# Turning the attention output by DMA for twelve tiles, with the low half on GpSimd

## The chip, the cores and the metric

The kernel runs on one core of one Trainium2 chip. The metric is the device time of one launch, in microseconds (us). The engines are named as the profile names them: PE (TensorE), DVE (VectorE), ACT (ScalarE), POOL (GpSimd) and SP (SyncE, which issues most of the DMAs); PEld is the loading of weights into PE.

## The reference

A transformer block on 2048 positions of width 512 in float32: attention over 8 keys, spaced two positions apart, in 32 heads of 16, then an MLP with a squared ReLU; each is preceded by a layer norm and followed by a residual add.

```python
qkv = layernorm(x) @ wqkv                    # 512 -> 3 * 512, 32 heads of 16
idx = pos[:, None] - arange(8)[None, :] * 2  # keys at s, s-2, ..., s-14
logits = einsum("bhsd,bhswd->bhsw", q, k[idx]) * 16 ** -0.5   # masked where idx < 0
o = einsum("bhsw,bhswd->bhsd", softmax(logits), v[idx])
h = x + o @ wo
r = relu(layernorm(h) @ w1 + b1)             # 512 -> 1792
out = h + (r * r) @ w2 + b2                  # 1792 -> 512
```

## The kernel before

**Tiles and halves.** The positions are 16 tiles of 128 (`t` = 0 to 15), in four groups of four (R = 4). Every matrix product is made of three products of half-precision parts: each operand is split into a high half (`hi`: a rounding copy on ACT, L147) and a low half (`lo`: operand minus high half, L150), and PE adds high x high, low x high and high x low in PSUM (`mm3`, 12 matmuls of 128x512 each). `lows_last` puts the products that need the low half of the first operand at the end, so that the eight others can go ahead of it.

**The chain of one tile.** Attention (DVE: products with the keys at L343, sums at L377, products with the values at L354, the latter added up on POOL by three instructions at L411) leaves its result `o`. This must be turned (transposed in blocks of 128x128) before `wo_product` can multiply it. There are two ways to turn it. `o_T` uses four PE transposes into PSUM. The other way goes by DMA: `o_split` copies the tile on ACT into two planes of 16 bits (`pl`, L594), `turn_dma` lets SP issue a transposing DMA (L598), and `o_join` puts the planes together again on ACT (L603). Either way `hi_T` then makes the high half `oh` on ACT and `lo_T` the low half `ol` on DVE. After `wo_product`, `h_add` (DVE, L639) adds the residual; statistics of the sum follow, either on DVE (`norm_stats`) or, for the tiles in `AS`, by three ACT instructions (`act_stats`), and three small POOL instructions (`finish` within them) finish both kinds. `h_norm` (ACT, L200) norms the sum into `hn`, which is turned for the MLP in the same two ways (tiles in `HV` by DMA), and `add_b2` (POOL) adds a bias to `h`.

`OV` names the tiles whose `o` goes by DMA, `HV` those whose `hn` does; before, both are 4, 5, 8, 9, 12, 13, the first two tiles of groups 1 to 3.

**Phases.** First the QKV products of all tiles; `first_phase` interleaves them with the first four tiles' attention results (tables `OT`, `WO`, `HT`, `HK`). Then three stages u = 0, 1, 2 of 17 slots each: a slot holds the first MLP product of a block of hidden units (`mlp1`, 12 matmuls) and the second of a block three slots earlier (`mlp2`), both for group u, while the chains of group u + 1 are threaded in by tables of slot numbers: `OP` (the turn of `o`), `WP` (`wo_product`), `HP`. Between them ACT makes the hidden block (`hidden`: ReLU, square, high half `rh`), and POOL its low half `rl`. The last group's MLP follows by itself.

**What sets the order.** Each engine runs its instructions in the order in which the program emits them. A slot emits its PE work, then what was put down for it by `at(delta, ...)`, then as many pieces of attention as a count of estimated DVE time allows (`pump`, times the factor in `SLOW` for the stage), then what was put down by `after(delta, ...)`:

```python
def end_slot(pe):
    now["pe"] += pe
    run(due)     # what at() put down
    pump()       # attention, as far as the estimated DVE time allows
    run(late)    # what after() put down
    now["slot"] += 1
```

So an `after` on POOL stands behind the sums of all attention pieces of that slot, and an `at` ahead of them.

Of the kernel before, what the change touches and what calls it, by code (L numbers as in the profile page):

```python
# [19 lines left out]
R = 4  # L20
RI = 2
# [8 lines left out]
ROWS = 15  # L30
LAG = 3
AS = (4, 5, 8, 9, 12, 13)
OV = (4, 5, 8, 9, 12, 13)
HV = (4, 5, 8, 9, 12, 13)
SLOW = 1.01, 1.10, 1.06
DELAY = 3
WJ = 2
XT = (9, 11), (7, 8)
OT = 4, 5, 10, 12
WO = 7, 9, 13, 15  # L40
HT = 20, 20, 21, 23
OK = (-6, -2, 4), (-5, -1, 5), (3, 6, 10), (4, 7, 12)
HK = (12, 15, 18), (14, 16, 19)
W2 = (18,)
LH = 3, 4, 10, 11
OP = 6, 7, 12, 13
# [12 lines left out]
def block_kernel(ctx, tc, x, wqkv, wo, w1, b1, w2, b2, out):  # L59
# [52 lines left out]
    def at(delta, fn, *a):  # L112
        due.setdefault(now["slot"] + delta, []).append((fn, a))

    def after(delta, fn, *a):
        late.setdefault(now["slot"] + delta, []).append((fn, a))
# [14 lines left out]
    def dve(t):  # L131
        now["dve"] += t
# [16 lines left out]
    def lo(eng, dst, src, h):  # L149
        eng.tensor_tensor(out=dst, in0=src, in1=h, op=ALU.subtract)  # L150
# [63 lines left out]
        for d, src in parts(tr, h_dst):  # L214
            hi(d, src)

    def lo_T(tr, h_dst, l_dst):
        for (d, src), h in zip(parts(tr, l_dst), h_dst):
            lo(nc.vector, d, src, h)
            dve(0.16 + 0.53 / len(h_dst))  # L220

    def mm3(ps, lh, ll, rh, rl, mid=None, at_=2 * KB, lows_last=False):

# [346 lines left out]
    def o_T(t):  # L570
        s, j = divmod(t, RI)
        pump(until=s)
        tr = transposes(o_t[s][:, j, :])
        if t % R == RI:

            ohl = att.tile([P, 2, KB, P], F32R, name="ohl", tag="o", bufs=3)
            oT[t] = ohl[:, 0], ohl[:, 1]
        else:
            oT[t] = row("oh", (P, KB, P), F32R), row("ol", (P, KB, P), F32R)
        at(0, hi_T, tr, [oT[t][0]])  # L580
        at(0, lo_T, tr, [oT[t][0]], [oT[t][1]])
# [30 lines left out]
    def o_join(t):  # L612
        turn_join(("o", t))
        tr = planes.pop(("o", t))
        if t % R == RI:
            ohl = att.tile([P, 2, KB, P], F32R, name="ohl", tag="o", bufs=3)
            oT[t] = ohl[:, 0], ohl[:, 1]
        else:
            oT[t] = row("oh", (P, KB, P), F32R), row("ol", (P, KB, P), F32R)
        hi_T(tr, [oT[t][0]])  # L620
        after(0, lo_T, tr, [oT[t][0]], [oT[t][1]])

    def h_split(t):
        turn_split(("h", t), hn.pop(t))
# [12 lines left out]
    def h_add(t, ps):  # L637
        h = hs[t]
        nc.vector.tensor_tensor(out=h, in0=ps, in1=h, op=ALU.add)  # L639
        dve(0.7)  # L640
        (act_stats if t in AS else norm_stats)(t, h)

    def h_norm(t):
        hn[t] = row("hn")
# [13 lines left out]
    def wo_product(t, slots):  # L658
        ps = turn["mm"].tile("wo")
        oh, ol = oT.pop(t)  # L660
        mm3(ps, lambda k: oh[:, k, :], lambda k: ol[:, k, :],
            lambda k: wo_h[:, k, :], lambda k: wo_l[:, k, :], lows_last=t in OV)
        for n, (fn, a) in zip(slots, ((h_add, (t, ps)), (h_norm, (t,)), (add_b2, (t,)),
                                      (spill, (t,)))):
            (after if fn in (h_norm, spill) else at)(n + (fn is add_b2), fn, *a)

# [311 lines left out]
    def first_phase(t0):  # L980
        def chores(m):
            if t0 + 3 < 16:
                if m in (0, 2):
                    at(0, x_stats, t0 + 2 + m // 2)

                early = t0 == 12
                if m + early in (6, 7):
                    at(0, x_norm, t0 - 4 + m + early)
                if m in XT[early]:
                    x_T(t0 + 2 + XT[early].index(m))  # L990
            if t0 + 5 < 16 and m in (6, 9):
                at(0, load_x, t0 + 2 + m // 3)
            if jobs and m % 3 == 0:
                at(0, weight_job)
            k = t0 // 2 * 12 - 72 + m
            if k == 19:
                dve(HOLD)
            for t in range(R):
                if k == OT[t]:
                    at(0, load_h, t)  # L1000
                    if t not in OV:
                        o_T(t)
                if t in OV and k in OK[t]:
                    at(0, (o_split, lambda t: turn_dma(("o", t)), o_join)[OK[t].index(k)], t)
                if t in HV and k in HK[t]:
                    at(0, (h_split, lambda t: turn_dma(("h", t)),
                           lambda t: turn_join(("h", t)))[HK[t].index(k)], t)
                if k == WO[t]:
                    wo_product(t, (1, 3, 4, 6))
                    now["pe"] += 2.73  # L1010
                if k == HT[t]:
                    (at(0, h_parts, t) if t in HV else h_T(t))
            if k in W2:
                at(0, load_w2, W2.index(k))

        def half(m):
            end_slot(1.37)
            chores(m)

        for n in range(6):  # L1020
            chores(2 * n)
            qkv_of(t0 + n % 2, n // 2, lambda: half(2 * n + 1))
            end_slot(1.37)
# [41 lines left out]
    for u in range(R - 1):  # L1065
        now["sub"] = u
        first, end = u == 0, False
        fs = list(range(FB)) if first else [*sorted(place), 12, 13]
        fs += [f for f in range(12) if f not in fs and (u < 2 or f not in ENDS)]
        fs += ENDS if u == 2 else []  # L1070
        need = [] if first else [f for f in fs if f < 12 and f not in place]
        acc = [psum.tile([P, D], F32, name="acc", tag=tag) for tag in ("acc0", "acc1", "tr0", "tr1")]
        js = range(R)


        todo, halves = {}, {}
        for i in js:
            t = R * (u + 1) + i
            if not end:
                a = i // 2 if u == 2 else 0  # L1080
                o0 = OP[i] - a
                if t in OV:
                    turned = [(o0, at, 0, o_split, t), (o0, after, 0, turn_dma, ("o", t)),
                              (o0 + 2, at, 0, o_join, t)]
                else:
                    turned = [(o0, o_T, t)]
                if t in HV:
                    h0 = 12
                    turned += [(h0, at, 0, h_split, t), (h0, after, 0, turn_dma, ("h", t)),
                               (h0 + 2, at, 0, turn_join, ("h", t))]  # L1090
                for p, *what in ((LH[i] - a, at, 0, load_h, t), *turned,
                                 (WP[i] - a, wo_product, t, (0, 1, 2 + 3 * a, 3 + 3 * a))):
                    todo.setdefault(p, []).append(what)
                p, h = (HP[i], i % 2) if u < 2 else HL[i]
                if t in HV:
                    todo.setdefault(p, []).append((at, 0, h_parts, t))
                else:
                    (todo, halves)[h].setdefault(p, []).append((h_T, t))
            todo.setdefault(UP[i], []).append((at, 0, unspill, R * u + i))
        if u == 2:  # L1100
            for p, *what in ((12, at, 0, t_load, 0), (12, at, 0, t_load, 1), (13, after, 0, t_sums, 0),
                             (13, after, 0, t_sums, 1), (13, at, 1, t_split, 0),
                             (14, after, 0, t_split, 1)):
                todo.setdefault(p, []).append(what)

        def half(p):
            run(due)
            for fn, *a in halves[p]:
                fn(*a)

        for p in range(FB + LAG):
            more = 0.0
            if p == FB:
                run(due)
                dve(HOLD)
            if u < 2 and p == FB - 2:
                dve(HOLD)
            for fn, *a in sorted(todo.get(p, []), key=lambda x: x[0] is wo_product):
                fn(*a)
                more += 2.73 if fn is wo_product else 0.0  # L1120
            if p < FB:
                mlp1(u, fs[p])
                more += 2.73
                if first:
                    at(0, split_w2, p)
                    if p + 1 < FB:
                        load_w2(p + 1)
            q = p - LAG
            if q >= 0:
                f = fs[q]  # L1130
                mlp2(u, f, acc, js, q == 0, q == FB - 1,
                     (lambda: half(p)) if p in halves else None)
                more += 2.74
                if f < 12 and (need or first and p < FB - LAG):
                    free.append(place.pop(f))
                    if need:
                        at(1, fetch, need.pop(0))
            end_slot(more)
        for i in js:
            at(u // 2, finish, R * u + i, acc[i])  # L1140
# [83 lines left out]
```

## Time and profile before

| | before |
|---|---|
| runs | 511.61, 512.64, 512.82 us; median 512.64 |
| profiled execution | 512.31 us; its span 510.5 us |
| granted PE clock | 0.999 |
| busy: PE, DVE, POOL, ACT | 501.9, 376.7, 351.2, 290.9 us |
| stages u = 0, 1, 2 begin | at 163.3, 252.5 and 343.2 us |

The profiled execution takes 1.81 us more than its span, which is the stretch from the first instruction that the profiler counts to the last. Busy time is a sum over instructions, and PE's ends are modelled, so two PE rows may overlap by a little. An entry `[0.61 <-DVE ol L150]` at the end of a timeline row says that the engine had been idle for 0.61 us, and what ended that.

### The profile page before, as it was taken

The page shows a single profiled execution, that of the slowest core. Times are in us where ns is not written, and L with a number is a line of the kernel's source. Part 1 is how long each engine was busy: PE and PEld are TensorE (multiplying, and loading weights), DVE is VectorE, ACT ScalarE, POOL GpSimd, SP SyncE. Part 2 cuts the span into 40 slices and gives each one's busy share as a digit, 9 for nine tenths or more (in the row PEclk, how much of TensorE's full clock was granted, in tenths as well). Part 3 has the DMA queues.
Part 4 walks back from the last instruction along what each step waited for, and adds up shares of the span by engine and source line. Part 5 has one row for each costly group of instructions (what it writes and reads, how often), then busy time and mean ns, then how long its engine had stood idle before and what let it go on. Part 6 is the DMA issues. An engine that isn't in the chain of part 4 may idle for free. (4 is left out here: it accounts for less than half of the span.)

```text
span 510.5 us, 7598 instructions
## 1 busy us (share of the span) xinstructions
PE 501.9 (98%) x2460; PEld 424.4 (83%) x2460; DVE 376.7 (74%) x512; ACT 290.9 (57%) x552; POOL 351.2 (69%) x430
## 2 busy tenths in 40 slices
PE   7999999999999999999999999999999999999997
PEld 6999788888888888888888878888888888998986
DVE  5479899988998899788879979899963046832233
ACT  4634686767434767485364557264564737666541
POOL 4714799895786798786778768776897364685610
PEclk9999999999999999999999999999999999999999
DMA  8678998989677889666587955767672172444112
GB/s 264 180 225 203 256 295 299 271 285 274 204 225 214 276 301 272 200 199 174 182 253 217 226 166 163 202 199 249 207 152 67 52 217 84 160 142 133 62 42 83
DMA packets 100912, 100.52 MB, mean 197 GB/s; under 512 B 21000, under 2 KB 69384, under 8 KB 100872
## 3 DMA queue, kind: packets, MB, share of 16 engines
q1 hardware_dynamic: 99928, 99.52, 65.4%
q10 hardware_dynamic: 944, 0.52, 0.3%
q8 instruction: 19, 0.31, 0.3%
q14 instruction: 21, 0.17, 0.1%
HBM read 72.65 MB, written 24.25 MB: 190 GB/s over the span
## 5 line engine op out<-in xcount | busy, mean ns | idle before, releaser
L411 POOL TENSOR_TENSOR pr<-pr 128x512 f32<-128x512 f32 (+1 forms) x128 | 132.5, 1035 | 45.7 <-DVE pr L354 40.3
L232 PE MATMUL mm<-big_l,w_h 128*128 128x512 f32 x336 | 88.7, 390 | 0.0
L354 DVE TENSOR_TENSOR pr<-ex,v 128x1024 f32<-128x1024 f32 x64 | 78.2, 1222 | 12.8 <-POOL o L411 6.5
L343 DVE TENSOR_TENSOR pr<-qp,k 128x1024 f32<-128x1024 f32 x64 | 76.9, 1202 | 5.6 <-ACT qp L272 5.5
L377 DVE TENSOR_REDUCE ex<-pr 128x64 f32<-128x1024 f32 x64 | 78.4, 1226 | 1.9
L232 PEld LDWEIGHTS mm<-big_l,w_h 128*128 128x128 f32 x336 | 62.8, 188 | 13.0
L150 POOL TENSOR_TENSOR rl<-r,rh 128x512 fp32r<-128x512 f32 x42 | 56.2, 1339 | 19.6 <-ACT rh L147 16.5
L232 PE MATMUL mm<-big_h,xl 128*128 128x512 f32 (+1 forms) x208 | 56.0, 379 | 0.2 <-DVE xl L150 0.2
L232 PE MATMUL mm<-big_h,xh 128*128 128x512 f32 (+1 forms) x208 | 53.5, 378 | 0.7 <-ACT xh L147 0.7
L232 PE MATMUL mm<-big_l,xh 128*128 128x512 f32 (+1 forms) x208 | 52.8, 375 | 0.0
L870 PE MATMUL acc<-big_l,rh 128*128 128x512 f32 x190 | 52.2, 390 | 0.0
L870 PE MATMUL acc<-big_h,rh 128*128 128x512 f32 x190 | 52.1, 391 | 0.0
L501 ACT COPY y<-mm 128x512 f32<-128x512 f32 (+1 forms) x52 | 28.6, 552 | 41.2 <-PE mm L232 33.0
L870 PE MATMUL acc<-big_h,rl 128*128 128x512 f32 x190 | 51.7, 389 | 0.0
L846 ACT ACTIVATE r<-mm,b_sb 128x512 f32<-128x512 f32 x42 | 28.8, 685 | 32.4 <-PE mm L232 32.3
L232 PE MATMUL mm<-big_l,w_l 128*128 128x512 f32 x168 | 45.0, 389 | 0.0
L232 PEld LDWEIGHTS mm<-big_h,xh 128*128 128x128 f32 x208 | 37.6, 188 | 7.0 <-ACT xh L147 1.5
L232 PEld LDWEIGHTS mm<-big_l,xh 128*128 128x128 f32 x208 | 38.2, 188 | 6.1 <-POOL big_l L150 0.2
L232 PEld LDWEIGHTS mm<-big_h,xl 128*128 128x128 f32 x208 | 37.2, 188 | 5.8 <-DVE xl L150 0.6
L870 PEld LDWEIGHTS acc<-big_h,rl 128*128 128x128 f32 x190 | 35.7, 188 | 7.5
L870 PEld LDWEIGHTS acc<-big_l,rh 128*128 128x128 f32 x190 | 35.5, 188 | 7.4
L870 PEld LDWEIGHTS acc<-big_h,rh 128*128 128x128 f32 x190 | 34.9, 188 | 6.7
(160 smaller groups left out, 904.1 us busy)
## 6 DMA issues: line engine op xcount, KB each, us to landing
k<-qkv_d SPq DMA_DIRECT2D x48, 288.0 KB, 2.8
v<-qkv_d SPq DMA_DIRECT2D x48, 288.0 KB, 3.2
qkv_d<-y SPq DMA_DIRECT2D x18, 512.0 KB, 4.2
big_l<-w2l_d SPq DMA_DIRECT2D x24, 256.0 KB, 3.0
xt<-in_A_x_dram SPq DMA_DIRECT2D x16, 256.0 KB, 4.6
q<-qkv_d SPq DMA_DIRECT2D x32, 128.0 KB, 4.7
h<-in_A_x_dram SPq DMA_DIRECT2D x16, 256.0 KB, 3.9
h_d<-h SPq DMA_DIRECT2D x16, 256.0 KB, 3.2
```

Source lines behind the costliest of these rows:

```text
L150: eng.tensor_tensor(out=dst, in0=src, in1=h, op=ALU.subtract)
L232: nc.tensor.matmul(ps, l(k), r(k), start=(n == 0), stop=(n == 3 * KB - 1))
L343: nc.vector.tensor_tensor(out=pr.rearrange("p i w h d -> p i w (h d)"), in0=qps["now"][:, j % 2].unsqueeze(2).to_broadcast([P, RI, W, GC]) ...
L354: nc.vector.tensor_tensor(out=p2, in1=vwin, op=ALU.mult, in0=e1[:, :, :, j * GH:(j + 1) * GH].unsqueeze(4).to_broadcast([P, RI, W, GH, DH]))
L377: nc.vector.tensor_reduce(out=lf[:, :, :, j * GH:(j + 1) * GH], in_=pr, axis=X, op=ALU.add)
L411: nc.gpsimd.tensor_tensor(out=dst, in0=p2[:, :, :w], in1=p2[:, :, w:2 * w], op=ALU.add)
L501: nc.scalar.copy(y[:, :, t % RI * GC:(t % RI + 1) * GC], ps[:, :j * GC].rearrange("p (j c) -> p j c", j=j))
L846: nc.scalar.activation(r, ps, AF.Relu, bias=b1_sb[:, f:f + 1])
L870: nc.tensor.matmul(acc[j], l[:, j * P:(j + 1) * P], w[f], start=(first and n < len(js)), stop=(last and n >= len(terms) - len(js)))
```

## The change

- All tiles of groups 1 to 3 have `o` turned by DMA (`OV` = 4 to 15), and tiles 0 and 1 have their `hn` turned by DMA too (`HV`), with table `HK` for the first phase cut to two entries.
- `lo_T` takes an engine, and `o_join` names POOL: `ol` is made on POOL, for tiles 4 to 11 behind the slot's attention (`after`), for 12 to 15 ahead of it (`at`).
- For the third and fourth tile of each group `o_split` stands two slots sooner than the table says, and its `turn_dma` one slot behind it.
- Since `wo_product` takes `lows_last` from `OV`, tiles 6, 7, 10, 11, 14 and 15 now have it.
- `act_stats` comes one slot after `h_add`; `h_norm` of these tiles comes one slot later and by `at`.
- `SLOW` goes from 1.10 and 1.06 to 1.08 and 1.04 in stages 1 and 2.

```diff
-OV = (4, 5, 8, 9, 12, 13)
-HV = (4, 5, 8, 9, 12, 13)
-SLOW = 1.01, 1.10, 1.06
+OV = tuple(range(4, 16))
+HV = (0, 1, 4, 5, 8, 9, 12, 13)
+SLOW = 1.01, 1.08, 1.04
...
-OK = (-6, -2, 4), (-5, -1, 5), (3, 6, 10), (4, 7, 12)
-HK = (12, 15, 18), (14, 16, 19)
+HK = (12, 18), (14, 19)
...
-    def lo_T(tr, h_dst, l_dst):
+    def lo_T(tr, h_dst, l_dst, eng=nc.vector):
         for (d, src), h in zip(parts(tr, l_dst), h_dst):
-            lo(nc.vector, d, src, h)
-            dve(0.16 + 0.53 / len(h_dst))
+            lo(eng, d, src, h)
+            if eng is nc.vector:
+                dve(0.16 + 0.53 / len(h_dst))
...
         hi_T(tr, [oT[t][0]])
-        after(0, lo_T, tr, [oT[t][0]], [oT[t][1]])
+        (after if t < 3 * R else at)(0, lo_T, tr, [oT[t][0]], [oT[t][1]], nc.gpsimd)
...
         dve(0.7)
-        (act_stats if t in AS else norm_stats)(t, h)
+        if t in AS:
+            at(1, act_stats, t, h)
+        else:
+            norm_stats(t, h)
...
-            (after if fn in (h_norm, spill) else at)(n + (fn is add_b2), fn, *a)
+            more = fn is add_b2 or fn is h_norm and t in AS
+            (after if fn in (h_norm, spill) and not (fn is h_norm and t in AS) else at)(
+                n + more, fn, *a)
...
-                o0 = OP[i] - a
+                o0 = OP[i] - a - (2 if i >= RI and t in OV else 0)
                 if t in OV:
-                    turned = [(o0, at, 0, o_split, t), (o0, after, 0, turn_dma, ("o", t)),
+                    turned = [(o0, at, 0, o_split, t), (o0, at if i >= RI else after, i // RI, turn_dma, ("o", t)),
                               (o0 + 2, at, 0, o_join, t)]
```

(In the first phase the turn of `hn` of tiles 0 and 1 is written with the two entries of `HK`: split and issue in the slot of the first, join in the slot of the second.)

What this does to the order is shown at two places of stage 1. The first is POOL around the `wo_product` of tiles 8 and 9. Before, this row of instructions holds only the low halves of the hidden block (`rl`), the three-instruction sums of attention (`pr`, `pr`, `o`) and the finish of tile 8's statistics (`rs`):

```order
L150 TENSOR_TENSOR rl_3383<-r_3381,rh_3382 128x512
L411 TENSOR_TENSOR pr_3400<-pr_3400 128x2x256
L411 TENSOR_TENSOR pr_3400<-pr_3400 128x2x128
L411 TENSOR_TENSOR o_3106<-pr_3400 128x2x64
L411 TENSOR_TENSOR pr_3412<-pr_3412 128x2x256
L411 TENSOR_TENSOR pr_3412<-pr_3412 128x2x128
L411 TENSOR_TENSOR o_3106<-pr_3412 128x2x64
L187 TENSOR_SCALAR rs_3394<-sq_3393 128x1
L189 TENSOR_TENSOR rs_3394<-rs_3394,mhalf_82 128x1
L190 TENSOR_TENSOR rs_3394<-nm_3392,rs_3394 128x1
L150 TENSOR_TENSOR rl_3464<-r_3462,rh_3463 128x512
```

In the changed program the same place of POOL reads:

```order
L149 TENSOR_TENSOR ol_3323<-pl_3210,oh_3322 128x512
L149 TENSOR_TENSOR rl_3387<-r_3385,rh_3386 128x512
L411 TENSOR_TENSOR pr_3401<-pr_3401 128x2x256
L411 TENSOR_TENSOR pr_3401<-pr_3401 128x2x128
L411 TENSOR_TENSOR o_3067<-pr_3401 128x2x64
L411 TENSOR_TENSOR pr_3411<-pr_3411 128x2x256
L411 TENSOR_TENSOR pr_3411<-pr_3411 128x2x128
L411 TENSOR_TENSOR o_3067<-pr_3411 128x2x64
L149 TENSOR_TENSOR ol_3393<-pl_3265,oh_3392 128x512
L149 TENSOR_TENSOR rl_3471<-r_3469,rh_3470 128x512
```

The low halves of tile 8 (`ol_3323`) and tile 9 (`ol_3393`) stand on POOL now, each behind the sums of its slot, and the finish of tile 8's statistics has left this place.

DVE shows where the products that these sums wait for stand, in the changed program (`h_3046` is tile 8's residual sum, which waits for tile 8's `wo_product`):

```order
L639 TENSOR_TENSOR h_3046<-wo_3347,h_3046 128x512
L343 TENSOR_TENSOR pr_3397<-qp_3330,k_3282 128x1024
L354 TENSOR_TENSOR pr_3401<-ex_226,v_3287 128x1024
L377 TENSOR_REDUCE ex_226<-pr_3397 128x16x4
L354 TENSOR_TENSOR pr_3411<-ex_226,v_3340 128x1024
```

Both products that `ol_3393` has ahead of it on POOL (`pr_3401`, `pr_3411`) are behind tile 8's residual add; before, DVE's row there is the next one, in which `ol` of tile 9 (`ol_3389`) is DVE's own and waits for no sum on POOL:

```order
L150 TENSOR_TENSOR ol_3317<-pl_3206,oh_3316 128x512
L639 TENSOR_TENSOR h_3042<-wo_3343,h_3042 128x512
L354 TENSOR_TENSOR pr_3400<-ex_226,v_3265 128x1024
L377 TENSOR_REDUCE ex_226<-pr_3336 128x16x4
L343 TENSOR_TENSOR pr_3408<-qp_3334,k_3323 128x1024
L354 TENSOR_TENSOR pr_3412<-ex_226,v_3328 128x1024
L377 TENSOR_REDUCE ex_226<-pr_3408 128x16x4
L150 TENSOR_TENSOR ol_3389<-pl_3258,oh_3388 128x512
```

The second place is POOL from the finish of tile 9's statistics to the low half of tile 10 (`ohl_3623`), in the changed program; before, tile 10 was turned on PE, and its low half was made on DVE:

```order
L186 TENSOR_SCALAR rs_3553<-sq_3552 128x1
L188 TENSOR_TENSOR rs_3553<-rs_3553,mhalf_82 128x1
L189 TENSOR_TENSOR rs_3553<-nm_3551,rs_3553 128x1
L652 TENSOR_TENSOR h_3046<-h_3046,b2_sb_81 128x512
L149 TENSOR_TENSOR rl_3613<-r_3611,rh_3612 128x512
L411 TENSOR_TENSOR pr_3575<-pr_3575 128x2x256
L411 TENSOR_TENSOR pr_3575<-pr_3575 128x2x128
L411 TENSOR_TENSOR o_3423<-pr_3575 128x2x64
L411 TENSOR_TENSOR pr_3632<-pr_3632 128x2x256
L411 TENSOR_TENSOR pr_3632<-pr_3632 128x2x128
L411 TENSOR_TENSOR o_3423<-pr_3632 128x2x64
L149 TENSOR_TENSOR ohl_3623<-pl_3485,ohl_3623 128x512
```

The low half of tile 10 is the last of this row: it stands behind two sums, a hidden block's low half and the finish of tile 9's statistics.

More of the change, by code (lines that the diff above doesn't have):

```diff
@@ L1000, in chores @@
                     at(0, load_h, t)
[L1001 to L1007, printed above, removed]
+                    o_T(t)
+                if t in HV and k == HK[t][0]:
+                    at(0, h_split, t)
+                    after(0, turn_dma, ("h", t))
+                if t in HV and k == HK[t][1]:
+                    at(0, turn_join, ("h", t))
                 if k == WO[t]:
```

## The prediction

> **What bounds the kernel now.** I read the page first. In it, busy time of PE stands at 98% of the span, with the granted clock at nine tenths or more in every slice:
>
> ```profile
> span 510.5 us, 7598 instructions
> PE 501.9 (98%) x2460; PEld 424.4 (83%) x2460; DVE 376.7 (74%) x512; ACT 290.9 (57%) x552; POOL 351.2 (69%) x430
> PEclk9999999999999999999999999999999999999999
> ```
>
> So the time is PE's work plus PE's waits, and an edit counts only if it takes instructions off PE or makes or ends a wait there. Next I read what PE waited for (us in total, times, longest). Where this change has its hand there is one such row:
>
> ```profile
> PE wo L232 <- DVE ol L150: 1.2, 2, 0.6
> ```
>
> The PE timeline shows both places, `wo_product` of tiles 8 and 9:
>
> ```profile
> 293.27 1.07 PE L232 MATMUL wo<-wo_h,oh 128*128 128x512 f32 x4
> 294.18 1.07 PE L232 MATMUL wo<-wo_l,oh 128*128 128x512 f32 x4
> 295.86 1.20 PE L232 MATMUL wo<-wo_h,ol 128*128 128x512 f32 x4 [0.61 <-DVE ol L150]
> 296.89 1.08 PE L232 MATMUL mm<-big_l,w_h 128*128 128x512 f32 x4
> ...
> 302.35 1.07 PE L232 MATMUL wo<-wo_h,oh 128*128 128x512 f32 x4
> 303.26 1.07 PE L232 MATMUL wo<-wo_l,oh 128*128 128x512 f32 x4
> 304.88 1.21 PE L232 MATMUL wo<-wo_h,ol 128*128 128x512 f32 x4 [0.56 <-DVE ol L150]
> ```
>
> These rows give the clockwork of a slot. Four matmuls go by each 0.91 us (293.27 to 294.18). The products with `ol` could have begun at 295.09 and began at 295.86: 0.77 lost. In tile 9 they could have begun at 304.17 and began at 304.88: 0.71 lost. Call E the moment at which PE has done a tile's `wo_product` and goes on (296.89 for tile 8). The next tile's begins 5.46 later (302.35) where it is in the next slot, and asks for its `ol` after eight matmuls, 1.82 later: at E + 7.28. Where two slots of 5.46 lie between (tiles 6 and 10) it is asked for at E + 18.2. After `ol` comes, PE needs about 1.03 to reach the next E. Every microsecond by which `ol` is later than that is added to the whole time, since PE has no slack to give it back from.
>
> **What comes off PE.** Tiles 6, 7, 10, 11, 14, 15 no longer have `o` turned on PE, tiles 0 and 1 no longer `hn`: 8 blocks of four transposes. The chain that ended last has one such block:
>
> ```profile
> 317.01 0.44 PE tr L205 x4
> ```
>
> 8 x 0.44 = 3.5 us off. If every `ol` came in time, the two waits (0.77 + 0.71 = 1.5) would go too: 5.0 us is all that the change can bring.
>
> **Where `ol` goes.** It leaves DVE, where it waits for nothing but `oh`, for POOL, behind the sums of the slot. DVE and POOL in stage 1, at tiles 8 and 9:
>
> ```profile
> 297.09 0.69 DVE L639 TENSOR_TENSOR h<-wo,h 128x512 f32<-128x512 f32 x1 [1.29 <-PE wo L232]
> 297.69 1.21 DVE L354 TENSOR_TENSOR pr<-ex,v 128x1024 f32<-128x1024 f32 x1
> 298.94 1.23 DVE L377 TENSOR_REDUCE ex<-pr 128x64 f32<-128x1024 f32 x1
> 300.08 1.22 DVE L343 TENSOR_TENSOR pr<-qp,k 128x1024 f32<-128x1024 f32 x1
> 301.68 1.22 DVE L354 TENSOR_TENSOR pr<-ex,v 128x1024 f32<-128x1024 f32 x1 [0.39 <-POOL o L411]
> ...
> 304.08 0.75 DVE L150 TENSOR_TENSOR ol<-pl,oh 128x512 fp32r<-128x512 f32 x1
> ```
>
> ```profile
> 295.21 1.74 POOL L150 TENSOR_TENSOR rl<-r,rh 128x512 fp32r<-128x512 f32 x1
> 298.99 2.12 POOL L411 TENSOR_TENSOR pr<-pr 128x512 f32<-128x512 f32 x2 [2.04 <-DVE pr L354]
> 301.18 0.47 POOL L411 TENSOR_TENSOR o<-pr 128x128 f32<-128x128 f32 x1
> 302.99 2.43 POOL L411 TENSOR_TENSOR pr<-pr 128x512 f32<-128x512 f32 x2 [1.34 <-DVE pr L354]
> 305.50 0.46 POOL L411 TENSOR_TENSOR o<-pr 128x128 f32<-128x128 f32 x1
> 306.04 0.19 POOL L187 TENSOR_SCALAR rs<-sq 128x1 f32<-128x1 f32 x1
> ...
> 306.94 0.19 POOL L190 TENSOR_TENSOR rs<-nm,rs 128x1 f32<-128x1 f32 x1
> ```
>
> The residual add of tile 8 waits for PE (0.20 behind E) and is done at E + 0.9. The slot's pieces of attention stand behind it on DVE, and the sum of the last product behind those on POOL: 2.65 us (298.99 to 301.65). Even in the kernel before that sum ends at 305.96, 1.8 us after PE could have used tile 9's `ol`. Now `ol` must come behind it, on an engine that takes longer (0.75 on DVE above). POOL's nearest row is the same subtraction with other names:
>
> ```profile
> L150 POOL TENSOR_TENSOR rl<-r,rh 128x512 fp32r<-128x512 f32 x42 | 56.2, 1339 | 19.6 <-ACT rh L147 16.5 <-issue 3.0
> ```
>
> I take this mean of 42, 1.34; its bounds are DVE's 0.75 and the 1.74 that the `rl` at 295.21 took, which moves a term by 0.6 at most.
>
> *Tile 9:* residual add 0.9, then four pieces of about 1.22 (keys, values, sum, values in the new order): E + 5.8; sum 2.65: 8.45; `ol` 1.34: 9.8. Asked for at 7.28: **2.5**. *Tile 5*, the same shape: **2.4** (a piece of it a little shorter).
>
> *Tile 7:* residual add 0.9, statistics on DVE 0.9, two pieces 2.45: 4.3; sum: 6.95; `ol`: 8.3. **1.0**.
>
> *Tile 11:* residual add 0.9, statistics 0.9, then the softmax's start of the next item, seven instructions from the sum of exponentials to the weighing of the values, which are in the same order at tile 10 before:
>
> ```profile
> 310.17 0.41 DVE L366 TENSOR_REDUCE sm<-ex 128x32 f32<-128x256 f32 x1
> ...
> 313.60 1.23 DVE L354 TENSOR_TENSOR pr<-ex,v 128x1024 f32<-128x1024 f32 x1
> ```
>
> They take 4.66 (310.17 to 314.83): E + 6.5; sum 9.1; `ol` 10.45: **3.2**.
>
> *Tile 10*, the longest, with E of tile 9. Residual add and these seven: E + 5.55; sum: 8.2. Behind it POOL finishes tile 8's statistics (306.04 to 307.13, 1.1): 9.3. This is where the later statistics cost: ACT has tile 8's `h_norm` ahead of the hidden block, and POOL's next `rl` needs that block. ACT's pieces, from the same stage before:
>
> ```profile
> 309.14 0.81 ACT L200 ACTIVATE hn<-h,rs 128x512 f32<-128x512 f32 x1
> 309.85 0.67 ACT L846 ACTIVATE r<-mm,b_sb 128x512 f32<-128x512 f32 x1
> 310.56 0.63 ACT L847 ACTIVATE r<-r 128x512 f32<-128x512 f32 x1
> 311.22 0.62 ACT L147 CAST rh<-r 128x512 fp32r<-128x512 f32 x1
> ```
>
> `h_norm` 0.8: 10.1; hidden 2.0 (309.85 to 311.84): 12.1; `rl`: 13.45; sum: 16.1; finish of tile 9: 17.2; `h_norm` and hidden again 2.8: 20.0 (`add_b2` on POOL lies beside it); `rl`: 21.4; two sums: 26.7; `ol`: 28.0. Asked for at 18.2: **9.8**. If ACT never held POOL up, POOL's own work from 8.2 on (two finishes 2.2, `add_b2` and two `rl` 4.0, three sums 7.95, `ol` 1.34) gives 23.7: 5.5 at least.
>
> *Tile 6* has the same kind of chain, since its split now stands two slots sooner and waits for that half of attention: POOL's sum to E5 + 1.6, split and exponential on ACT to 3.65, the seven DVE instructions to 8.4, sum, finish, `h_norm`, hidden, `rl`, sum, `ol` to 20.2: **2.0**, with bounds 0 and 3, as ACT may run ahead. *Tile 8*, where POOL has an `rl` and two sums ahead of `ol`: how far DVE lags behind PE there sets it; 0.77 lost before, **1.2** now, bounds 0 and 4.5. *Tile 12*, by `at`, whose `wo_product` begins 40.8 behind the stage's start (343.2) and asks for `ol` 42.6 behind it:
>
> ```profile
> 384.03 1.07 PE L232 MATMUL wo<-wo_h,oh 128*128 128x512 f32 x4
> ```
>
> POOL has ten sums, eight `rl`, a finish, an `add_b2` and `ol` ahead of that: 26.5 + 10.7 + 2.5 + 1.3 = 41.0, from some 2.3 behind the stage's start: **0.7** late, bounds 0 and 3. Tiles 4, 13, 14, 15: **0**; attention is over by tile 13, and tile 4 is the first of its stage, so that no residual add holds its sums.
>
> **What I cost at nothing.** ACT gains eight splits and eight joins:
>
> ```profile
> L594 ACT COPY pl<-o 128x1024 uint16<-128x1024 uint16 x6 | 6.2, 1040 | 0.0
> L603 ACT COPY pl<-o 128x1024 uint16<-128x1024 uint16 x6 | 7.0, 1168 | 1.3 <-DMA o<-pl 1.3
> ```
>
> That is 8 x 2.2 = 17.7 us on an engine busy 57%; outside the chains above PE never asks for it, and where it did, a split would cost at most its 1.0. SP's eight more transposing DMAs land in the time that these did (median us from issue to landing):
>
> ```profile
> o<-pl SPq DMA_TRANSPOSE x6, 4.3
> hn<-pl SPq DMA_TRANSPOSE x6, 5.1
> ```
>
> The joins come a slot of 5.46 or more behind the issue; in the first phase (tiles 0, 1) the join is four slots or more behind: 0, at most 0.3 each. Behind those issues on SP stand loads of keys and values, which are two pieces ahead. `SLOW`, 1.10 to 1.08, emits 2% more attention per slot, 1.8 us of the stage's 90.7: between 0.5 more and 0.5 less on tile 8 or 12. DVE gets 12 low halves lighter; it shortens no chain above, as each starts at a residual add.
>
> **The sum.** Waits: 2.4 + 2.0 + 1.0 + 1.2 + 2.5 + 9.8 + 3.2 + 0.7 = 22.8. Less 3.5 (transposes) and 1.5 (old waits): +17.8. The profiled execution took 512.31, 0.33 under the median of 512.64. 512.31 + 17.8 = 530.1; against the median, **530.4**.
>
> **Rivals.**
>
> *B: POOL's order costs, but ACT never holds it.* ACT has finished `h_norm` and hidden early, and tile 10 waits 5.5. With tiles 6, 8 and 12 at 0: 2.4 + 1.0 + 2.5 + 5.5 + 3.2 = 14.6, less 5.0: 522. For it: ACT is busy 57% only. Against: with the statistics a slot later, POOL's finish of tile 8 and the `h_norm` that waits for it meet the very hidden block whose `rl` POOL must do next.
>
> *C, the other side: all lows arrive in time*, and the 5.0 come off: 512.64 - 5.0 = 507.6. It decides where a slot's last product on DVE ends by E + 3.3 (7.28 - 2.65 - 1.34). For it: POOL is not full, as stage 1 shows (busy of PE, PEld, DVE, ACT, POOL):
>
> ```profile
> 252.50:343.20 90.70, 89.53 (x401) 73.45 (x400) 79.19 (x95) 50.14 (x89) 69.80 (x81) 1.00 0.71 203
> ```
>
> 69.80 and four `ol` of 1.34 are 75 of 90.70. Against: that product ended at E + 6.0 in the trace (302.90), and it can't move ahead of a residual add that waits for PE.
>
> *D: worse.* Tiles 6, 8 and 12 at their upper bounds (+1.0, +3.3, +2.3): 537. The clock may join in. The start shows it: 24 transposes after idleness took 353 ns each, later ones 273:
>
> ```profile
> L918 PE MATMUL tr<-ident 128*128 128x128 f32 x24 | 4.2, 353 | 1.3 <-POOL mhalf L904 1.3
> L205 PE MATMUL tr<-ident,hn 128*128 128x128 f32 x36 | 5.3, 273 | 0.0
> ```
>
> That was 1.9 us over, so a PE that goes cold in tile 10's wait loses about 2 more: 539. The Trainium skill, "TensorE: Matmul & The Clock Gate", section "What's actually happening", says that an idle window of some 3.4 us halves the clock, and that as long a busy one restores it; the estimate by it is 1.7 us more behind any wait that long, 532.1 in place of 530.4. The trace has no wait in mid-kernel long enough to try it.
>
> **Chances.** My sum 0.60; B 0.20; C 0.06; D 0.12; nothing to be seen, the waits just paying for the 5.0, 0.02. The measurement can tell about 0.3% (1.5 us) from no change. The range reaches from below B, with tile 7 at 0 and tile 10 short of its 5.5 by two, 519, to D with the clock, 541. Faster 0.06, same 0.02, slower 0.92.
>
> **What would show it.** In the changed kernel's trace PE waits for `ol` on POOL in tiles 5, 7, 9, 11 by 1 to 3 us and in tile 10 by 5 to 10, with no waits in 13 to 15; POOL's `ol` directly behind a sum that ended beyond E + 8; ACT's `h_norm` of tile 8 waiting for POOL's finish. I am wrong if tile 9's `ol` is there within 7.3 us of tile 8's E, or if tile 10 waits less than 4.

## The result, and the profile after

The changed kernel takes 541.59 us (four runs, 539.38 to 542.70) against 512.31 (511.61 to 512.82): 1.057 times as long, interval 1.053 to 1.060. The direction was forecast; the size, +29 us, was not: the time lies 0.6 us above the range's upper end of 541 and 11 above the forecast of 530.4. The profiled execution took 541.62 us, with a span of 539.5 against 510.5 before.

The page of the changed kernel (span, busy time, granted PE clock by slices):

```profile
span 539.5 us, 7576 instructions
PE 506.3 (94%) x2428; PEld 424.7 (79%) x2428; DVE 370.6 (69%) x500; ACT 307.5 (57%) x568; POOL 364.2 (68%) x442
PEclk8999999999999999999999899799999999999999
```

PE has 32 transposes fewer to do and yet waits far longer: 94% busy in place of 98%. Its busy time did not fall by the 3.5 us of the transposes, in part at least because some matmuls ran at a lower clock (the 8 at the start and the 8 and the 7 past the middle of the clock row). What PE waited for, in the view of the waits (us in total, times, longest):

```profile
PE wo L232 <- POOL ol L149: 11.5, 6, 2.9
PE wo L232 <- ACT ohl L146: 9.9, 2, 7.1
PE tr L204 <- ACT hn L199: 1.8, 1, 1.8
PE tr L705 <- ACT hn L199: 1.4, 1, 1.4
PE mm L232 <- ACT y L501: 0.7, 1, 0.7
```

The first row is the wait that the prediction was about, now on POOL and six times. The second is tiles 6 and 10, where `ohl` is the high half (the low half is made in the same tile). PE's timeline at tiles 8 to 10, the places of the prediction's rows:

```profile
305.78 2.08 PE L232 MATMUL wo<-wo_h,ol 128*128 128x512 f32 x4 [2.73 <-POOL ol L149]
307.66 1.65 PE L232 MATMUL mm<-big_l,w_h 128*128 128x512 f32 x4
...
317.46 1.20 PE L232 MATMUL wo<-wo_h,ol 128*128 128x512 f32 x4 [1.79 <-POOL ol L149]
...
342.17 2.07 PE L232 MATMUL wo<-wo_h,ohl 128*128 128x512 f32 x4 [7.06 <-ACT ohl L146]
344.04 1.91 PE L232 MATMUL wo<-wo_l,ohl 128*128 128x512 f32 x4
346.29 1.24 PE L232 MATMUL wo<-wo_h,ohl 128*128 128x512 f32 x4 [0.35 <-POOL ohl L149]
```

Tile 10's chain is all there in POOL's and ACT's timelines. POOL:

```profile
326.23 0.46 POOL L411 TENSOR_TENSOR o<-pr 128x128 f32<-128x128 f32 x1
...
327.68 0.19 POOL L189 TENSOR_TENSOR rs<-nm,rs 128x1 f32<-128x1 f32 x1
330.69 1.29 POOL L149 TENSOR_TENSOR rl<-r,rh 128x512 fp32r<-128x512 f32 x1 [2.82 <-ACT rh L146]
...
338.59 1.27 POOL L149 TENSOR_TENSOR rl<-r,rh 128x512 fp32r<-128x512 f32 x1 [1.59 <-ACT rh L146]
...
344.97 1.27 POOL L149 TENSOR_TENSOR ohl<-pl,ohl 128x512 fp32r<-128x512 f32 x1
```

and ACT:

```profile
327.90 0.81 ACT L199 ACTIVATE hn<-h,rs 128x512 f32<-128x512 f32 x1 [5.19 <-POOL rs L189]
...
335.82 0.81 ACT L199 ACTIVATE hn<-h,rs 128x512 f32<-128x512 f32 x1 [2.56 <-POOL rs L189]
...
338.42 1.99 ACT L594 COPY pl<-hn 128x1024 uint16<-128x1024 uint16 x2
340.31 1.15 ACT L603 COPY pl<-o 128x1024 uint16<-128x1024 uint16 x1
341.50 0.62 ACT L146 CAST ohl<-pl 128x512 fp32r<-128x512 f32 x1
```

The two engines take turns: the sum on POOL ends, the finish of the statistics follows (327.68), ACT's norm has waited 5.19 us for it, the hidden block stands behind the norm, POOL's `rl` waits 2.82 us for that, and so once more. With PE's E of tile 9 at 318.49, the prediction had the sum's end at E + 8.2 (it came at 8.2), the second hidden block's `rl` done at 21.4 (at 21.4) and `ol` at 28.0 (at 27.75).

### The profile page after: what moved, and what is told of

It reads as the page before. It is cut to its first block, busy times and chain, and to the rows that moved or that the text cites. A ratio compares the mean times of both kernels' runs of the same rounds, so it can differ in the third digit from the quotient of the medians.

```text
span 539.5 us, 7576 instructions
## 1 busy us (share of the span) xinstructions
PE 506.3 (94%) x2428; PEld 424.7 (79%) x2428; DVE 370.6 (69%) x500; ACT 307.5 (57%) x568; POOL 364.2 (68%) x442
## 5 line engine op out<-in xcount | busy, mean ns | idle before, releaser
L149 POOL TENSOR_TENSOR rl<-r,rh 128x512 fp32r<-128x512 f32 x42 | 54.3, 1296 | 28.4 <-ACT rh L146 24.7
L639 DVE TENSOR_TENSOR h<-wo,h 128x512 f32<-128x512 f32 x16 | 11.0, 686 | 62.8 <-PE wo L232 49.8
```

## Experiments

All times are medians; the kernel before stood at 511.8 to 512.1 beside them, and each ratio is to it. Three parts of the change are told apart: **L** (low half on POOL), **S** (statistics and norm a slot later) and **T** (late tiles turned by DMA). What is left over, tiles 0 and 1 and `SLOW`, are "the small edits".

**One part undone.** `low_dve` makes the low half on DVE:

```diff
-        (after if t < 3 * R else at)(0, lo_T, ..., nc.gpsimd)
+        after(0, lo_T, tr, [oT[t][0]], [oT[t][1]])
```

> The changed kernel with the low half of the attention result made on VectorE again (all else as changed). Theory 'queue' (the low halves wait in GpSimd's order behind sums that a residual add holds up): the waits for them at tiles 5, 7, 8, 9, 11 and 12 (2.6, 1.0, 2.9, 2.0, 3.1, 1.0 us, 12.6 in all) go, up to the 1.5 us that the kernel before has; the waits for the high half at tiles 6 and 10 (3.0 and 7.2) stay in the main: about 528 us. Theory 'statistics' (the late statistics make ScalarE hold the hidden blocks and joins): within 3 us of the changed kernel, 539 to 542.

521.38 us, ratio 1.018 (1.016 to 1.020): 20 us less, where "queue" said about 14. Its waits:

```profile
PE wo L232 <- ACT ohl L146: 7.3, 2, 4.3
PE wo L232 <- DVE ol L149: 2.5, 3, 1.5
```

The waits on POOL are gone, and tile 10's for the high half fell as well, from 7.2 to 3.1. The turns of POOL and ACT are as long as they were: from the end of POOL's finish of tile 8 to the high half 14.25 us in both kernels. But the finish ends 5.2 us behind tile 9's E here (316.99, E at 311.80) and 9.4 in the changed kernel (327.87, E at 318.49). Tile 6's wait rose to 4.5.

`low_at` leaves `ol` on POOL, but ahead of the slot's sums for all tiles (`at` in place of `after`):

> The changed kernel with the low half on GpSimd, but ahead of the slot's sums for all twelve tiles, not only for tiles 12 to 15. Theory 'queue': what costs is the place behind the sums, not the engine: the waits at tiles 5, 7, 8, 9 and 11 fall from 11.6 us to under 2 in all, tiles 6 and 10 keep waiting for the high half: 528 to 532 us. If it is GpSimd's speed or load, the waits stay within a third of what they are: 537 or more.

527.68 us, ratio 1.030 (1.029 to 1.032): 14 us less, 0.3 below what "queue" gave. The waits for low halves fell to one of 0.8, at tile 12:

```profile
PE wo L232 <- ACT ohl L146: 10.6, 2, 7.1
PE wo L232 <- POOL ol L149: 0.8, 1, 0.8
```

The same twelve `ol` are on the same engine; only the place of eight of them (tiles 4 to 11) differs. So the place behind the sums costs these 11 us of waits; the 6 us between this kernel and `low_dve` are what POOL's doing it may cost.

`stats_back` puts S back:

```diff
-        if t in AS:
-            at(1, act_stats, t, h)
-        else:
-            norm_stats(t, h)
+        (act_stats if t in AS else norm_stats)(t, h)
...
+            (after if fn in (h_norm, spill) else at)(n + (fn is add_b2), fn, *a)
```

> The changed kernel with ScalarE's statistics and the norm that follows put back to where they were before (one slot sooner). Theory 'queue': tile 10 loses the part of its wait that comes of ScalarE standing for the norms (7.2 to some 3 us, and the slow clock behind it goes), tiles 5, 7, 9, 11 keep theirs: about 535 us. Theory 'statistics': the norms are the main cost; tiles 6 and 10 wait under 1 us, the late waits of the transposes (2.0 and 1.6) go too: 528 us or less.

534.45 us, ratio 1.044 (1.042 to 1.047): the time is what "queue" gave, with the waits at tiles 5, 7, 8 and 9 as they were. Tile 11's fell from 3.1 to 1.4, which "queue" did not have. Tile 10 no longer waits for the high half but 4.1 us for the low one, on POOL. Tile 6 kept 3.0, and ACT's timeline shows one thing that the prediction had not seen:

```profile
235.92 1.04 ACT L594 COPY pl<-hn 128x1024 uint16<-128x1024 uint16 x1 [2.48 <-PE acc L870]
236.87 1.15 ACT L603 COPY pl<-o 128x1024 uint16<-128x1024 uint16 x1
238.06 0.62 ACT L146 CAST ohl<-pl 128x512 fp32r<-128x512 f32 x1
```

The split of tile 5's norm waits for PE to be done with the slot's last `mlp2` (probably for a buffer, which the planes share with `rl`), and tile 6's join stands behind it on ACT: 1.04 + 1.15 + 0.62, and PE waits just that much.

`ov_back` puts T back (`OV` of six tiles):

> The changed kernel with one part undone: the third and fourth tile of each group turned on PE again (the low halves of the six DMA tiles stay on GpSimd, the statistics stay late). If the late tiles' way over DMA is a cost of its own: clearly under the changed kernel's 541.6, 531 or less. If the parts work through one queue (GpSimd's), so that PE waits for a hidden block in place of a high half: 533 to 541, no nearer to 512 than 20 us.

537.13 us, ratio 1.049 (1.048 to 1.051): the second theory's time. Waits for high halves can't come any more, and PE waits 11.3 us for hidden blocks (`mm <- ACT r`) instead.

**One part alone.** `pool_only` is the kernel before with `nc.gpsimd` in the one `lo_T` of `o_join`, behind the sums; `pool_only_at` the same with `at`, ahead of them:

> The kernel before with one edit: the low halves of its six tiles that go by DMA are made on GpSimd behind the slot's sums. Theory 'queue': tiles 5 and 9 wait 2 to 2.6 us, tile 8 from 1.2 to 2.9, less the 1.5 that they wait before: 517 to 519 us. Theory 'statistics', or that moving the late tiles to DMA is what costs: 512 to 514.

> The kernel before with the low halves of its six DMA tiles on GpSimd, ahead of the slot's sums; the same edit behind the sums took 522.9, with waits of 1.4, 3.6 and 3.5 at tiles 5, 9 and 12. If the place in the queue is what costs: these three fall under 0.8 each, 511 to 514 us. If GpSimd's load or speed is what costs: they stay over half, 517 or more.

522.89 us, ratio 1.021 (1.020 to 1.023), and 517.08, ratio 1.010 (1.008 to 1.012). Both are above what "queue" said. Their waits, of `pool_only` first:

```profile
PE wo L233 <- POOL ol L150: 7.9, 3, 3.4
```

```profile
PE wo L233 <- POOL ol L150: 3.3, 1, 3.3
PE mm L233 <- ACT r L847: 1.6, 1, 1.6
```

Behind the sums tiles 5, 9 and 12 wait 1.4, 3.6 and 3.5 us; ahead of them tiles 5 and 9 don't, tile 12 still does (3.4). So the place explains tiles 5 and 9, not tile 12; the time of 517.08 by itself would also fit the other theory. At tile 12 the other theory is right, for there POOL is behind with its work. In `pool_only_at` it works without a pause from 370.55 on, DVE waits for it, and the last sum begins 2.2 us after its product was done (381.31 to 383.47); `ol` stands behind that sum and an `rl`, while PE could have used it at 385.19:

```profile
377.04 1.22 DVE L355 TENSOR_TENSOR pr<-ex,v 128x1024 f32<-128x1024 f32 x1 [1.68 <-POOL pr L412]
...
383.47 2.10 POOL L412 TENSOR_TENSOR pr<-pr 128x512 f32<-128x512 f32 x2
...
387.28 1.26 POOL L150 TENSOR_TENSOR ol<-pl,oh 128x512 fp32r<-128x512 f32 x1
```

`dve_ov` has S and the small edits, with L and T undone:

> The changed kernel with two other parts undone: the low half on VectorE, and the third and fourth tile of each group turned on PE again; the late statistics stay. The 9.3 us of waits for the high halves of tiles 6 and 10 can't come any more, six blocks of transposes (2.6 us) come back: 514 to 515 us. If the late statistics cost by themselves (the norm holding the hidden block), PE waits for hidden blocks or low halves around tiles 6 and 10 instead: 517 or more.

529.18 us, ratio 1.034 (1.033 to 1.036): the second branch. The late statistics cost by themselves:

```profile
PE mm L232 <- ACT r L851: 8.9, 2, 4.8
PE wo L232 <- DVE ol L149: 2.5, 1, 2.5
```

ACT's norm stands ahead of the hidden block whose ReLU frees the bank that PE wants:

```profile
229.14 0.81 ACT L199 ACTIVATE hn<-h,rs 128x512 f32<-128x512 f32 x1 [3.00 <-POOL rs L189]
229.86 0.67 ACT L851 ACTIVATE r<-mm,b_sb 128x512 f32<-128x512 f32 x1
```

`finish_early` is that kernel with POOL's finish of ACT's statistics ahead of the slot's sums:

```diff
-        after(0, finish)
+        finish()
```

> The kernel with late statistics but PE turning and the low half on VectorE (529.2 us), with one edit: the finish of ScalarE's statistics on GpSimd ahead of the slot's sums. Theory 'queue': the norm on ScalarE, and with it the hidden block that PE waits for (8.9 us, and the slow clock of 2 to 3 us behind it), is held by the sums that the finish stands behind: 514 to 518 us. Theory 'ScalarE's load': the waits for the hidden block stay over half: 524 or more.

516.44 us, ratio 1.010 (1.008 to 1.011): as "queue" had it. The statistics are as late and ACT does as much; PE's waits for hidden blocks are gone, and the time is no longer than that of the small edits alone (`hv_slow` below, 516.77). So S costs by the same thing as L, small POOL instructions behind sums.

`dve_stats` undoes L and S and keeps T:

> The changed kernel with two parts undone: the low half on VectorE, and ScalarE's statistics and norms where they were before. With the low half alone undone it takes 521.4, and still waits for the high halves of tiles 6 (4.5, and 1.7 of slow clock behind it) and 10 (3.1). Theory 'join behind splits' (tile 6's join stands on ScalarE behind the copies of the normed residuals, the second of which waits for a buffer until PE has done the slot ahead of tile 6): tile 6 keeps about 3.0, tile 10 gets under 1.5: 516 to 518 us. Theory 'statistics' (the late statistics alone hold ScalarE): both go, 512 to 513.

517.23 us, ratio 1.011 (1.009 to 1.013): in the range of "join behind splits", but not by its numbers: tile 6 waits 2.2 for the high half, not 3.0, and tile 10 still 0.7 for the high half and 2.3 for the low one. `dve_stats_join` puts the join ahead of the splits in that slot:

```diff
-sorted(todo.get(p, []), key=lambda x: x[0] is wo_product)
+sorted(todo.get(p, []), key=lambda x: (x[0] is wo_product, len(x) > 2 and x[2] is h_split))
```

> As the kernel with both parts undone (low half on VectorE, statistics where they were), and besides it the join of tiles 6, 10 and 14 is put ahead of the copies of the normed residuals on ScalarE. Theory 'join behind splits': tile 6's wait for the high half falls from about 3.0 to under 0.5, nothing else changes: 2.5 to 3.5 us less than without it, 513 to 515. Theory 'statistics': no difference to the kernel without it beyond 1 us.

518.07 us, ratio 1.012 (1.009 to 1.015): a miss. Tile 6's wait for the high half fell to 1.0, but 0.8 for the low half follows it; tile 10's for the low half rose from 2.3 to 3.1, and tile 12 waits 1.9 in place of 0.9. The join's place holds tile 6 for about 1 us and is worth nothing alone.

**The small edits.** `hv_slow` has only them, with L, S and T undone; `hv_only` only tiles 0 and 1 by DMA; `slow_back` is the changed kernel with the factors of before (`SLOW = 1.01, 1.10, 1.06`).

> Only what is left of the change when its three large parts are undone: tiles 0 and 1 of the normed residual by DMA, and the two factors of the attention count. Two blocks of transposes off (0.9 us), one wait of 0.85 us for ScalarE's copy at the start of stage 0 on: 511.5 to 512.5 us, no difference that can be told. If the factors matter, tiles 8 and 9 wait up to 1 us more or less.

> The kernel before with tiles 0 and 1 of the normed residual by DMA, and nothing else. If the factors are what makes the small edits cost 4.7 us: two blocks of transposes off (0.9), one wait of 0.85 for ScalarE's copy on: 511.6 to 512.6 us, tile 8 waiting 0.8. If the DMA way of these two tiles is: 514 or more.

> The changed kernel with the factors of the attention count put back to 1.10 and 1.06. If the factors are behind tile 8's wait (2.9 us and 0.8 of slow clock, where the prediction had 1.2): it falls under 1.5, and the time to 537 to 539 us. If not: 541 to 542, tile 8 as it was.

516.77 us, ratio 1.009 (1.008 to 1.011); 516.38, ratio 1.008 (1.007 to 1.009); 538.69, ratio 1.052 (1.050 to 1.053). What was expected of `hv_slow` was wrong by 4 us. Of the two branches for `hv_only` the second holds, 514 or more: taking these two tiles off PE costs by itself. `slow_back` came out as its first branch said. In `hv_slow` tile 8 waits 3.1 us for its low half, in `hv_only` tile 9 waits 3.9. The reason can be read from DVE's timeline of `hv_only`, beside the rows of before in the prediction:

```profile
295.34 0.69 DVE L639 TENSOR_TENSOR h<-wo,h 128x512 f32<-128x512 f32 x1 [1.90 <-PE wo L232]
298.24 1.23 DVE L343 TENSOR_TENSOR pr<-qp,k 128x1024 f32<-128x1024 f32 x1 [2.20 <-ACT qp L272]
...
304.48 1.77 DVE L150 TENSOR_TENSOR ol<-pl,oh 128x512 fp32r<-128x512 f32 x1
```

Two blocks of transposes less are 0.9 us less in the program's count of PE time, by which `pump` decides how many pieces of attention a slot gets. So one product with the keys has slipped from ahead of tile 8's residual add (293.69 before, the add at 297.09) to behind it. There it waits 2.2 us for its query, which ACT copies behind the statistics of that same residual. Five pieces of attention stand between the add and tile 9's `ol`, as many as before, so `ol` begins 2.2 later behind E; it also takes 1.77 in place of 0.75 (last section). With the 0.7 lost before, that is the 3.9.

In `hv_slow` the slip goes the other way, at tile 8: a product with the values that stood behind the add before (297.69) now stands ahead of `ol`, a query comes 0.61 late, and the subtraction takes 1.51:

```profile
294.43 1.22 DVE L343 TENSOR_TENSOR pr<-qp,k 128x1024 f32<-128x1024 f32 x1 [0.61 <-ACT qp L272]
295.57 1.21 DVE L354 TENSOR_TENSOR pr<-ex,v 128x1024 f32<-128x1024 f32 x1
296.70 1.51 DVE L149 TENSOR_TENSOR ol<-pl,oh 128x512 fp32r<-128x512 f32 x1
```

In the changed kernel the factors alone move waits between tiles: with those of before (`slow_back`) tile 8 waits 1.45 in place of 2.9 and tile 11 nothing in place of 3.1, while tile 6 waits 3.8 in place of 3.0 and tile 12 waits 3.5 in place of 0.95; in all the kernel is 3 us faster.

**Everything kept, the order mended.** `low_at_finish` is the changed kernel with L and S and T in it, and two lines of POOL's order: `ol` by `at`, and `finish()` at once.

> The changed kernel with its whole work kept and only GpSimd's order mended at two places: the low half ahead of the slot's sums (that alone: 527.7), and the finish of ScalarE's statistics ahead of them too. Theory 'queue': tile 10's 7.2 falls under 2, the late waits of the transposes (2.0 and 1.6) go, tile 6 keeps about 3 for its buffer: 516 to 519 us. If the loads of GpSimd and ScalarE are what costs: tiles 6 and 10 keep over half of their 11 us, 523 or more.

517.57 us, ratio 1.013 (1.010 to 1.015): "queue" again. 24 of the 29 us go, with the same work on the same engines. The longest waits that are left where the change has its hand:

```profile
PE wo L232 <- ACT ohl L146: 2.8, 1, 2.8
PE tr L204 <- ACT hn L199: 2.2, 1, 2.2
```

Tile 10 has no wait left, tile 6 keeps its 3.0, tile 12 its 1.0. One thing did not go as expected: PE's transposes of `hn` in stage 1 (tile 11) still wait 2.2. Tile 11's statistics are made on DVE, and the edit moved only the finish of ACT's; POOL still finishes tile 11's behind a sum, and ACT's norm waits for that:

```profile
342.60 0.52 POOL L411 TENSOR_TENSOR o<-pr 128x128 f32<-128x128 f32 x1
...
344.57 0.81 ACT L199 ACTIVATE hn<-h,rs 128x512 f32<-128x512 f32 x1 [3.89 <-POOL rs L167]
```

**A version that beats both.** `before_at` is the kernel before with one word changed, VectorE's low halves ahead of the slot's attention:

```diff
-        after(0, lo_T, tr, [oT[t][0]], [oT[t][1]])
+        at(0, lo_T, tr, [oT[t][0]], [oT[t][1]])
```

> The kernel before with the low half of its six DMA tiles on VectorE ahead of the slot's attention, not behind it. Its two waits of 0.77 and 0.71 us at tiles 8 and 9 go: 510.5 to 511, 0.3% faster. If VectorE then waits for the high half at the cost of attention, a later tile waits for it: 512 or more.

510.85 us against 512.07, ratio 0.998 (0.997 to 0.999): 1.2 us faster, about what the two waits were; they are not in its list any more:

```profile
PE tr L918 <- POOL mhalf L904: 1.3, 1, 1.3
PE mm L232 <- ACT xh L147: 0.7, 1, 0.7
```

## Why the prediction was right in direction and short in size

| step | forecast | measured in the changed kernel |
|---|---|---|
| `ol` late, tiles 5, 7, 9, 11 | 2.4, 1.0, 2.5, 3.2 | 2.6, 1.0, 2.0 + 0.6 slow clock, 3.1 |
| tile 10 | 9.8 | 9.7 |
| tile 6 | 2.0 | 3.0 |
| tile 8 | 1.2 | 2.9 + 0.9 slow clock |
| tile 12 | 0.7 | 0.95 |
| tiles 4, 13 to 15 | 0 | 0 |
| transposes off PE | -3.5 | -3.3 |
| old waits | -1.5 | -1.5 |
| transposes of `hn` (tiles 11, 15) | not priced | 2.0, 1.6 |
| ACT's copy ahead of stage 0 | 0 | 0.85 |
| the first 20 us | 0 | 1.65 |

Measured waits are what PE's instructions began later than the ones ahead of them allow; slow clock is what four matmuls took over those of before. Both slow clocks come behind tile 8's wait; the second four matmuls (307.66 to 309.15) made PE ask for tile 9's `ol` 0.6 later, and `ol` came 9.75 behind E, where the prediction had 9.8. Tile 10's is from 318.49 to 347.37, where PE went on, less the 19.1 of its own work between. The rows give +28 of the +29 us between the spans; the rest was not followed up. The first 20 us ran at a granted clock of 0.91 in this one profile; in the fifteen experiments' profiles they took what they took before, within 0.2, so that this row belongs to the execution and not to the change.

*Right:* the place of `ol` behind sums that a residual add holds, at tiles 5, 7, 9 and 11; tile 10's turns of POOL and ACT; the late statistics as what makes them; tile 12 as a matter of POOL's load. `low_at`, `finish_early` and `low_at_finish` show that elsewhere it is the order on POOL. That the parts don't add up is shown too: the late tiles by DMA cost 4.5 us beside L and S (537.13 to 541.59), 0.5 with neither (516.77 to 517.23, no difference that can be told), and with S alone they save 7.8 (529.18 to 521.38).

*The steps that failed.* First, tile 8's term, mis-sized by 2.5 (though inside its own bounds of 0 and 4.5), and with it the sentence that costs `SLOW` and the first phase "at nothing": both edits move the line between one slot's attention and the next, and a piece that slips across a residual add costs whole microseconds. Alone they cost 4.7 (`hv_slow`). Second, the prediction followed ACT's norm only up to the low halves: late norms of tiles 11 and 15 make PE's own transposes wait, 3.6 in all. Tile 11's norm waits for POOL's finish, which stands behind a sum (ended at 365.71, the norm began at 367.15). Tile 15's does not: its finish was done at 450.19, but on ACT the norm (455.18) stands behind a hidden block, two joins and this copy, which itself had waited for POOL:

```profile
448.68 1.05 ACT L146 CAST th<-traw 128x1024 fp32r<-128x1024 f32 x1 [4.87 <-POOL traw L769]
```

Third, at tile 6 only the low half was followed; the high half, which ACT joins behind the splits and PE asks for first, was the one that came late. At tile 10 too it is the high half that PE waits 7.1 us for, but there `ol` came last, so the term held.

The range was missed by little: without any one of tile 8's 2.5, the 3.6 of the transposes or the 1.65 of the first 20 us, the table's sum would have stayed inside. The forecast of 530.4 was missed by what these rows add up to. The range's upper end was also not what its text gives: D with the clock is 537 and 2, that is 539, so 2 of the 541 have no term.

*The clock.* In the windows of the changed kernel from 304 to 320 and from 341 to 350 us the granted clock (third column from the right) is 0.89 and 0.70:

```profile
304.00:320.00 16.00, 12.42 (x47) 9.87 (x48) 8.57 (x11) 6.94 (x13) 10.33 (x11) 0.89 0.46 149
341.00:350.00 9.00, 7.49 (x24) 5.54 (x25) 3.55 (x6) 5.18 (x9) 7.43 (x9) 0.70 0.80 110
```

At tile 10 four matmuls took twice their time (342.17 to 344.04, 1.87 and not 0.91), the next four hardly less, and cost nothing, since the last four had to wait for `ol` anyway. The Trainium skill's "TensorE: Matmul & The Clock Gate", section "What's actually happening", whose rule would have added 1.7 us there by the prediction's estimate, agrees on the drop; the 1.7 were hidden. The row by which the prediction saw the clock at the start (353 ns for each of 24 transposes) does not show it: the trace of before gives a granted clock of 1.00 from 1.3 to 5.6 us, where they ran.

## What to carry to other kernels

An instruction that a bottleneck engine waits for should be priced by what stands ahead of it in its own engine's queue, and by what that in turn waits for: here twelve instructions of 1.3 us on an engine 68% busy cost 20 us beside the change's other parts, and with eight of them a few places sooner they cost 6. Where a counter deals out filler work by estimated time, a small edit to the count is not free: look up which piece slips across which wait. And follow a held instruction to all who wait for it, not to the one that the change is about.

## What was not expected of the hardware

The clock fell after 2.73 us of idle PE at tile 8 (four matmuls in 2.08, then 1.65, normal from 309.15 on), but not after 2.84 at tile 6 or 2.92 at tile 11, whose matmuls came at 0.91 for four. In `slow_back` it fell after 2.47 us at tile 6, with another wait of 1.03 just ahead (granted 0.72 from 240 to 246 us), and not after 3.32 at tile 12 (1.00 from 407 to 416). So in these traces the length of a single wait does not tell whether the clock falls. The section of the Trainium skill named above says that the window of some 3.4 us runs freely; that a wait shorter than it can drop the clock, as it did here, is beyond what that section says.

The same 128x512 subtraction on DVE took 0.75 us at tile 9 before and 1.77 in `hv_only`, where POOL's `rl` (304.44 to 305.71) ran beside it:

```profile
304.44 1.27 POOL L150 TENSOR_TENSOR rl<-r,rh 128x512 fp32r<-128x512 f32 x1
```

Three more low halves that began just behind an `rl` and ran beside it took 1.76 to 1.79 (`low_dve` 393.80, `hv_slow` 393.18, `dve_stats_join` 391.18). Where DVE began first it is POOL that took longer, as in `dve_ov`:

```profile
313.29 0.78 DVE L149 TENSOR_TENSOR ol<-pl,oh 128x512 fp32r<-128x512 f32 x1
...
313.48 1.74 POOL L149 TENSOR_TENSOR rl<-r,rh 128x512 fp32r<-128x512 f32 x1
```

So in these rows the one that begins second pays, by 0.5 to 1 us.
